# Four or five key tiles of each layer offered to VectorE, and a planner with other durations

## The chip, the cores and the metric

The kernel runs on one core of a Trainium2 chip. The metric is the device time of one execution in microseconds, as the median of several runs. Five engines take part, each with its own instruction queue that it works through in order: TensorE (PE, with its weight loads listed as PEld), VectorE (DVE), ScalarE (ACT), GpSimd (POOL) and SyncE (SP, which issues the DMAs). They wait for each other on semaphores.

## The reference

Two transformer layers with the same weights, over 2048 tokens of width 512, in bfloat16. Each layer is an attention block of 32 heads of 16 and a dense block of width 1792, each behind a layer norm and added to its input:

```python
qkv = (x @ wqkv).reshape(B, S, 3, H, Dh).transpose(2, 0, 3, 1, 4)
q, k, v = qkv[0], qkv[1], qkv[2]
scores = jnp.einsum("bhqd,bhkd->bhqk", q, k) * (Dh ** -0.5)
o = jnp.einsum("bhqk,bhkd->bhqd", softmax(scores), v)
attn = o.transpose(0, 2, 1, 3).reshape(B, S, D) @ wo
dense = gelu(x @ w1 + b1) @ w2 + b2          # gelu by its tanh form
...
x = x + A(layernorm(x)); x = x + B(layernorm(x))     # twice
```

## The kernel before

**The work.** The scores are cut into cells. A cell is the product of 128 keys with 512 query columns of one head: one matmul of 32 rows (two heads share the rows, and the queries of the other head are masked to zero by POOL into `qp`). A pass is one group of four cells per key tile (`a` from 0 to 3, one for each 32-row quarter of PE) over the key tiles of one segment of queries; with all 16 key tiles it has 64 cells. There are 4096 cells in the two layers. For each cell the exponential is taken and the result is multiplied with the values of that head, extended by a column of ones that sums the denominator; the products of a pass add up in PSUM bank 5 (`PVB`). When a pass ends, DVE and POOL divide and transpose its result (`norm`, L718).

**Two ways to an exponential.** PSUM has eight banks of 512 columns. ACT works in two slots, banks 0 to 2 and banks 3 and 4: one score instruction group of PE fills a slot with up to three or two cells, one ACT instruction (L1466) takes the exponential of the whole slot and writes it into as many exp buffers of the `pt` ring, and one value product per cell (L1527) reads it. The ring has `PT_RING` buffers (L24); parts of `k1`, `q` and `v0` join it while they are out of use. Some cells go to DVE instead. DVE turns a score into the bit pattern of a bfloat16 by one multiply and add (`dfirst`, L1283, from banks 6 and 7, or from bank 2). That pattern is a coarse exponential, linear between powers of two. To smooth it, `dchain` makes three more patterns of it, shifted by a fixed number (L1344 makes one, L1346 two; mostly for two cells at once), and all four are multiplied with values: the first with `v`, the other three with copies of it that POOL has scaled by the weights `VW` (`vcopies`, L1060, the instruction on L1068). So a cell on DVE costs four value products, not one. There are nine buffers for cells on DVE (`DU`), and two more late in layer 1.

**Which cells.** `KD` (L45) names for each layer the key tiles whose cells may go to DVE, and `NKD` (L46) sizes the room of the scaled copies. The others always go to ACT; what DVE has not taken by the end of a pass goes to ACT too (`next_act`, L1140). No cell goes to DVE before the scaled copies of all the tiles named for layer 0 are made (`lend` leaves 2 at the end of `vcopies`), nor in the first eight passes, which cover key tiles 0 to 3 alone.

**The order of everything** is made ahead by a list scheduler, `_Sched`, with a model of time. Threads yield operations with a cost in microseconds; the scheduler keeps a clock for each engine, picks the operation that can start first (by priority where several can), and sets its end to start, cost and a latency of its engine (`LATENCY`, L205). A change of PE's mode between scores and the four-way column products (mode "P") costs `SW`. The times themselves do not get into the program, only the order of each engine's queue, and the semaphore waits that the data need. Three decisions are made by the model's clocks when a score instruction is placed: `attach` (L1215) adds cells for DVE to it, if bank 7 or 6 is free within `TOL` of its start and DVE has a buffer; `swap` (L1192) gives the third bank of slot 0 to DVE, if the model's DVE clock is no more than `SWAP` ahead; and the `slack` of a score instruction lets PE run value products ahead of it, as long as it is not held up by more than 0.3 us, or by more where ACT is busy longer with the other slot:

```python
ahead = 0.065 + 0.4267 * self.held[1 - sl]
op = _Op("pe", MM, fns, reads=reads, writes=writes, mode="S", slack=max(SLACK, ahead - LATE))
```

Where PE would stand idle, `fill` (L312) puts in matmuls on the copies whose result nobody reads (L1125); `free` (L1090) chooses the bank that they write to, bank 5 with zero weights among them.

The lines that the prediction speaks of, beside those above: L1137 scores, L512 the projections and the dense block on PE, L683 the copy of projected values into `v`, L734 and L739 to L743 the evacuation of a pass.

Of the kernel before, what the change touches and what calls it, by code (L numbers as in the profile page):

```python
# [20 lines left out]
PVB = 5  # L21
MISC = (6, 7)
DBANK = (7,)
PT_RING = 19  # L24
LEND = (3, 2)
QP_RING = 3
W_RING = 4
# [14 lines left out]
JB = 0.64  # L42
JS = 0.025
EARLY = 4
KD = ((4, 5, 6, 7), (0, 1, 2, 12))  # L45
NKD = 4  # L46
TAIL = 10
OPENING = 18
ROUNDS = 2
# [152 lines left out]
        self.done = False  # L202


LATENCY = {"pe": 0.20, "act": 0.103149, "dve": 0.099491, "pool": 0.153328, "sp": 0.1}  # L205


class _Sched:
# [90 lines left out]
        return max(self.end.get(self.P.lastw[k], 0.0) if k in self.P.lastw else 1e9 for k in keys)  # L299

    def _cost(self, op):
        return op.cost + (SW if op.eng == "pe" and op.mode != self.mode else 0.0)

    def active(self, t):
        while self.stream and self.stream[0][1] < t - WINDOW:
# [6 lines left out]
    def fill(self, start, nxt):  # L312
        while self.filler and self.mode:
# [17 lines left out]
            self.clock["pe"] = now + into + MM + cold  # L331
            self.end[ev] = self.clock["pe"] + LATENCY["pe"]

    def run(self):
        while True:
# [53 lines left out]
            self.clock[e] = start + cost  # L389
            self.end[ev] = start + cost + op.tail + LATENCY[e]  # L390


SW = 0.107
# [3 lines left out]
def bass_interleave_layers__mha_block__dense_activation_gelu__prompt_kernel(  # L397
# [15 lines left out]
    with ExitStack() as es:  # L413
        def sb(shape, dt, name):
            return es.enter_context(nc.sbuf_tensor(name, shape, dt))
# [15 lines left out]
        T["WQKV"] = T["G"][:, 0:12, :].rearrange("p (w c) d -> p w c d", w=3)  # L431
        pt = sb([128, PT_RING, 512], BF16, "pt")
        T["PT"] = [pt[:, :, :]] + [T["K"][1][:, :, 512 * c:512 * c + 512] for c in LEND]
# [10 lines left out]
        T["DU"].append(late.rearrange("p (i j q) -> p i j q", i=4, j=2))  # L444
        T["VC"] = sb([128, NKD, 3, H * 17], BF16, "vc")
        T["XT"] = sb([128, 512], F32, "xt")
# [55 lines left out]
class _Plan:  # L502
# [530 lines left out]
    def setup_attention(self):  # L1033
# [4 lines left out]
        for pi, (l, seg, g, kts, part, final) in enumerate(self.pas):  # L1038
            self.alist.append([(pi, kt, a) for kt in kts if kt not in KD[l] for a in range(4)])
            self.dlist.append([(pi, kt, a) for kt in kts if kt in KD[l] for a in range(4)])  # L1040
            self.left.append(4 * len(kts))
# [18 lines left out]
    def vcopies(self):  # L1060
        T = self.T
        for l in range(NL):
            yield ("cond", lambda l=l: self.pv >= self.lead[l])
            for j, kt in enumerate(KD[l]):
                yield ("need", ("V", l, kt, kt // 4))
# [24 lines left out]
    def free(self, now, ahead):  # L1090
        P = self.P
        best = (None, 1e9)
        src = self.source()
        for b in (6, 7, 0, 1, 2, 3, 4, 5) if src else ():
            k = "B.%d" % b
            if k in ahead or b in self.hold or k in P.lastw and not P.reads.get(k) and P.lastw[k] not in self.s.fills:
                continue
            t = max([0.0] + [self.s.end.get(ev, 0.0) + FOLD for ev in P.deps(src, [k]) if ev[0] != "pe"])
            if max(t, now) < max(best[1], now):
                best = (b, t)  # L1100
        k = "B.%d" % PVB
        if best[1] > now and self.pvopen and "VC.0.0" in P.lastw and k not in ahead:
            best = (PVB, 0.0)
        return best
# [65 lines left out]
    def take(self, c, free):  # L1170
        self.scored += 1
        self.left[c[0]] -= 1
        if self.left[c[0]] == 0:
            free.append(self.s.tokens[("qp", c[0])])

    def join(self, op, d, b, extra, free):
        pools = self.s.pools
        if self.open is None:
            self.open = {"du": pools["du"].pop(0), "cells": [], "full": False}
        pair = self.open  # L1180
        pair["cells"].append(d)
        extra.append((d, b, pair, len(pair["cells"]) - 1))
        if len(pair["cells"]) == self.cap[pair["du"]]:
            self.open = None
        f, r = self.score(d, self.s.tokens[("qp", d[0])], b)
        op.fns.append(f)
        op.reads += r
        op.writes.append("B.%d" % b)
        self.take(d, free)
        self.nd += 1  # L1190
# [141 lines left out]
    def dchain(self, pair):  # L1332
# [16 lines left out]
        for jj, (pi, kt, a) in enumerate(cells):  # L1349
            l, seg, g = self.pas[pi][:3]  # L1350
            gb, ts = self.heads(seg, g)
            j = KD[l].index(kt)
            for i in range(4):
# [26 lines left out]
    def setup_units(self):  # L1380
        self.blocks, self.alias, self.closed = [(0, PT_RING)], {}, set()
        for c in LEND:
            lo = self.blocks[-1][1]
            self.blocks.append((lo, lo + NDC))
            for i in range(NDC):
                self.alias[lo + i] = ["K1.%d.%d" % (i, c)] + ["XL.%d" % t for t in range(4 * c, 4 * c + 4)]
        self.qblocks = len(self.blocks)
        for c in range(self.NQ):
            lo = self.blocks[-1][1]
            self.blocks.append((lo, lo + NDC))  # L1390
            for i in range(NDC):
                self.alias[lo + i] = ["Q.%d.%d" % (i, c)]
        lo = self.blocks[-1][1]
        self.blocks.append((lo, lo + 16))
        for i in range(16):
            self.alias[lo + i] = ["PART.1.%d" % (i // 2)]
# [163 lines left out]
    def run(self):  # L1560
# [6 lines left out]
        s.pool("s", range(len(SLOTS)))  # L1567
        s.pool("pt", range(PT_RING))
        self.setup_units()
# [52 lines left out]
```

## Time and profile before

| | us |
|---|---|
| median of 3 runs (1586.61 to 1589.74) | 1588.72 |
| span of the profiled execution | 1584.3 |
| ACT idle in the span (1584.3 - 1545.8) | 38.5 |
| DVE idle in the span (1584.3 - 1355.7) | 228.6 |
| PE idle in the span (1584.3 - 1432.2) | 152.1 |
| DVE's exponentials: L1283 (du, dh, kt) | 484.5 + 63.0 + 55.5 |
| POOL's scaled copies: 24 of 0.665 | 16.0 |

The profile is one execution on the chip. For each group of instructions it gives the engine, the line, the tiles written and read, the count, the busy time, the mean duration of one, and how long the engine stood idle just before, with what released it. Records of one engine can overlap; busy time counts an overlap once. The records of PE are modelled at their end and overlap most. The granted clock of TensorE is 0.998 on average.

### The profile page before, as it was taken

The page shows a single profiled execution, that of the slowest core. Times are in us where ns is not written, and L with a number is a line of the kernel's source. Part 1 is how long each engine was busy: PE and PEld are TensorE (multiplying, and loading weights), DVE is VectorE, ACT ScalarE, POOL GpSimd, SP SyncE. Part 2 cuts the span into 40 slices and gives each one's busy share as a digit, 9 for nine tenths or more (in the row PEclk, how much of TensorE's full clock was granted, in tenths as well). Part 3 has the DMA queues.
Part 4 walks back from the last instruction along what each step waited for, and adds up shares of the span by engine and source line. Part 5 has one row for each costly group of instructions (what it writes and reads, how often), then busy time and mean ns, then how long its engine had stood idle before and what let it go on. Part 6 is the DMA issues. An engine that isn't in the chain of part 4 may idle for free.

```text
span 1584.3 us, 43090 instructions
## 1 busy us (share of the span) xinstructions
PE 1432.2 (90%) x18795; PEld 447.9 (28%) x18795; DVE 1355.7 (86%) x2558; ACT 1545.8 (98%) x1392; POOL 200.9 (13%) x250
## 2 busy tenths in 40 slices
PE   8998889999999898998989989888898889889988
PEld 3222222222222222322222222222222222333344
DVE  5689999779998889989799789999789978988894
ACT  7999999999999999999999999999999999999995
POOL 5200011010110201002110020122002000010000
PEclk9999999999999999999999999999999999999999
DMA  5100001341014211152111521001251006213420
GB/s 141 22 1 2 1 16 34 95 126 43 22 48 135 80 41 28 42 149 66 35 28 48 159 50 35 1 14 28 84 151 43 26 9 174 82 36 101 142 82 29
DMA packets 141768, 96.90 MB, mean 61 GB/s; under 512 B 36877, under 2 KB 141582, under 8 KB 141582
## 3 DMA queue, kind: packets, MB, share of 16 engines
q1 hardware_dynamic: 141582, 94.14, 21.2%
q8 instruction: 150, 2.46, 0.6%
q14 instruction: 36, 0.29, 0.1%
HBM read 84.41 MB, written 2.10 MB: 55 GB/s over the span
## 4 chain that ended last, share of the span: by engine, by line
ACT 65%; PE 30%; DVE 2%; POOL 1%; DMA 1%; issue 1%; SPq 0%; POOLq 0%; ACTq 0%
ACT pt L1466 58%; PE ps L512 12%; PE ps L1137 9%; PE ps L1527 9%; ACT g L893 2%; ACT v L1466 1%; ACT kt L1466 1%; ACT q L1466 1%; DVE du L1283 1%; ACT L893 1%; PE ps L1125 1%; DMA xf<-xln 1%; DVE du L1346 0%; ACT L1466 0%; DVE du L1344 0%
## 5 line engine op out<-in xcount | busy, mean ns | idle before, releaser
L1466 ACT ACTIVATE pt<-ps 128x1536 bf16<-128x1536 f32 (+1 forms) x1264 | 1387.1, 1259 | 10.5 <-PE ps L1137 6.4
L1137 PE MATMUL ps<-qp,kt 32*128 32x512 bf16 x4096 | 534.7, 384 | 129.9 <-ACT pt L1466 91.5
L1283 DVE TENSOR_SCALAR du<-ps 128x512 uint16<-128x512 f32 x716 | 484.5, 686 | 92.7 <-PE ps L1137 85.9
L1527 PE MATMUL ps<-pt,v 128*17 128x512 bf16 (+1 forms) x3386 | 444.9, 359 | 3.2 <-DVE v L739 1.1
L1137 PEld LDWEIGHTS ps<-qp,kt 32*128 32x128 bf16 x4096 | 141.2, 91 | 677.1 <-ACT pt L1466 286.1
L1527 PE MATMUL ps<-du,vc 128*17 128x512 bf16 (+1 forms) x2403 | 326.6, 359 | 1.3 <-DVE du L1344 0.6
L1346 DVE TENSOR_SCALAR du<-du 128x2048 uint16<-128x2048 uint16 (+1 forms) x361 | 246.7, 686 | 2.2
L1085 POOL TENSOR_SCALAR qp<-q,mask 128x512 bf16<-128x512 bf16 (+1 forms) x91 | 66.9, 735 | 1005.5 <-PE ps L1137 996.4
L512 PE MATMUL ps<-xf,wr 128*32 128x512 bf16 (+1 forms) x2400 | 171.2, 369 | 3.0 <-DMA xf<-xln 1.6
L1344 DVE TENSOR_SCALAR du<-du 128x1024 uint16<-128x1024 uint16 (+1 forms) x361 | 152.6, 433 | 2.2
L1527 PE MATMUL ps<-du,v 128*17 128x512 bf16 (+1 forms) x801 | 148.3, 360 | 0.8 <-DVE du L1346 0.5
L1527 PEld LDWEIGHTS ps<-pt,v 128*17 128x17 bf16 x3386 | 114.4, 88 | 114.8 <-issue 76.6
L512 PE MATMUL ps<-wr,g 128*32 128x512 bf16 x1600 | 123.2, 386 | 3.9 <-ACT g L893 3.2
L1527 PEld LDWEIGHTS ps<-du,vc 128*17 128x17 bf16 x2403 | 91.0, 89 | 65.4 <-issue 30.2
L872 DVE TENSOR_SCALAR g<-ps,hb1t 128x512 bf16<-128x512 f32 (+1 forms) x112 | 79.9, 713 | 15.3 <-PE ps L512 13.9
L1527 PE MATMUL ps<-dh,vc 128*17 128x512 bf16 (+1 forms) x309 | 86.4, 357 | 0.0
L1283 DVE TENSOR_SCALAR dh<-ps 128x512 uint16<-128x512 f32 x92 | 63.0, 685 | 9.3 <-PE ps L1137 7.9
L512 PEld LDWEIGHTS ps<-xf,wr 128*32 128x32 bf16 x2400 | 52.5, 95 | 61.9 <-issue 33.6
L1283 DVE TENSOR_SCALAR kt<-ps 128x512 uint16<-128x512 f32 x81 | 55.5, 685 | 14.9 <-PE ps L1137 13.9
L602 POOL TENSOR_SCALAR xln<-x,rstd,nmr 128x512 bf16<-128x512 bf16 x58 | 56.3, 973 | 30.9 <-DMA xf<-xln 21.6
L1125 PE MATMUL ps<-vc 128*32 128x512 bf16 x520 | 54.7, 384 | 0.0
L754 POOL TENSOR_TENSOR ott<-xt,rc 128x256 bf16<-128x256 f32 x42 | 33.3, 792 | 164.3 <-DVE rc L746 158.8
(93 smaller groups left out, 1184.5 us busy)
## 6 DMA issues: line engine op xcount, KB each, us to landing
wr<-in_B_w_dram SPq DMA_DIRECT2D x256, 256.0 KB, 2.8
wr<-in_A_wqkv_dram SPq DMA_DIRECT2D x24, 256.0 KB, 2.9
wr<-in_A_wo_dram SPq DMA_DIRECT2D x18, 256.0 KB, 2.9
out_dram<-x SPq DMA_DIRECT2D x16, 128.0 KB, 2.6
g<-in_A_wqkv_dram SPq DMA_DIRECT2D x3, 512.0 KB, 6.0
x<-in_A_x_dram SPq DMA_DIRECT2D x3, 512.0 KB, 8.8
q<-in_B_w_dram SPq DMA_DIRECT2D x3, 512.0 KB, 5.5
kt<-in_B_w_dram SPq DMA_DIRECT2D x4, 256.0 KB, 3.3
```

The costliest lines, as they stand in the source:

```text
L512: return [lambda e, a=a: e.matmul(out[32 * a:32 * a + 32, :], lhsT=lhsT[:, 32 * a:32 * a + 32], rhs=rhs, start=start, stop=stop, tile_posi ...
L602: yield _Op(eng, cost, lambda e: e.tensor_scalar(T["XLN"][:, x, :], T["X"][:, t, :], T["RSTD"][:, t:t + 1], T["NMR"][:, t:t + 1], op0=ALU. ...
L872: yield _Op("dve", 0.21 + n / 966, lambda e, fc=fc, pb=pb: e.tensor_scalar(T["G"][:, fc, q], pb, T["HB1T"][:, fc:fc + 1], None, op0=ALU.ad ...
L893: lambda e, g=g: e.activation(out=g, in_=g, func=ACT.Gelu_apprx_tanh), reads=gk, writes=gk, prio=2)
L1085: yield _Op("pool", 0.1 + 0.6 * w / 512, lambda e, s=s, q=q, i=i, t=t, w=w: e.tensor_scalar(T["QP"][:, s, w * i:w * i + w], q, T["MASK"][: ...
L1125: fns.append(lambda e, o=o, w=w, a=a, m=m: e.matmul(o, lhsT=w, rhs=rhs, start=start, stop=start, tile_position=(0, m * a)))
L1137: return (lambda e: e.matmul(o, lhsT=lhsT, rhs=rhs, start=True, stop=True, tile_position=(32 * a, 0)), ["K%d.%d.%d" % (l, gb, kt // 4), "Q ...
L1283: yield _Op("dve", 0.68, lambda e: e.tensor_scalar(u, self.bank(b), E_SCALE, E_BIAS, op0=ALU.mult, op1=ALU.add), reads=["B.%d" % b], write ...
L1344: yield _Op("dve", 0.08 + 0.14 * n, lambda e: e.tensor_scalar(U[:, 1, 0:n, :], U[:, 0, 0:n, :], SHIFT, None, op0=ALU.add), reads=key[0], w ...
L1346: yield _Op("dve", 0.08 + 0.28 * n, lambda e: e.tensor_scalar(U[:, 2:4, 0:n, :], U[:, 0:2, 0:n, :], 2 * SHIFT, None, op0=ALU.add), reads=k ...
L1466: yield _Op("act", 0.065 + 0.4267 * n, lambda e, src=src, dst=dst: e.activation(out=dst, in_=src, func=ACT.Exp, scale=0.25), reads=["B.%d" ...
L1527: op.fns.append(lambda e, o=o, lhsT=q[0][0][m], rhs=q[0][1][:, n * m:n * m + n], a=a, st=st, sp=sp: e.matmul(o, lhsT=lhsT, rhs=rhs, start= ...
```

## The change

The planner gets other durations: larger latencies for PE, ACT and DVE; 0.083 us less for each DVE operation (at least 0.07 is left); 2% more for a PE operation of mode "P". A fifth key tile of each layer may go to DVE: tile 8 in layer 0, tile 3 in layer 1. Its three scaled copies take 3 x 544 x 2 = 3264 bytes of each partition; three buffers of the exp ring, 3 x 1024 = 3072 bytes, are given up. In `free`, bank 5 is no longer in the list of banks that filler matmuls may take; the rule behind the loop, which allows bank 5 in the middle of a pass, stays.

```diff
-PT_RING = 19
+PT_RING = 16
...
-KD = ((4, 5, 6, 7), (0, 1, 2, 12))
-NKD = 4
+KD = ((4, 5, 6, 7, 8), (0, 1, 2, 3, 12))
+NKD = 5
...
-LATENCY = {"pe": 0.20, "act": 0.103149, "dve": 0.099491, "pool": 0.153328, "sp": 0.1}
+LATENCY = {"pe": 0.219, "act": 0.21, "dve": 0.139, "pool": 0.153328, "sp": 0.1}
+OVERLAP = 0.083
+ROUND = 1.02
...
     def _cost(self, op):
-        return op.cost + (SW if op.eng == "pe" and op.mode != self.mode else 0.0)
+        if op.eng == "dve":
+            return max(op.cost - OVERLAP, 0.07)
+        if op.eng == "pe":
+            return op.cost * (ROUND if op.mode == "P" else 1.0) + (SW if op.mode != self.mode else 0.0)
+        return op.cost
...
-        for b in (6, 7, 0, 1, 2, 3, 4, 5) if src else ():
+        for b in (6, 7, 0, 1, 2, 3, 4) if src else ():
```

## The prediction

> **What bounds the kernel now.** I read the page's busy shares first, then its chain, its groups of instructions, the stretches by engine, the engines' own timelines and last the list of waits. The page's head and its chain:
>
> ```profile
> span 1584.3 us, 43090 instructions
> PE 1432.2 (90%) x18795; PEld 447.9 (28%) x18795; DVE 1355.7 (86%) x2558; ACT 1545.8 (98%) x1392; POOL 200.9 (13%) x250
> ...
> ACT 65%; PE 30%; DVE 2%; POOL 1%; DMA 1%; issue 1%; SPq 0%; POOLq 0%; ACTq 0%
> ```
>
> ACT is at work in all but 38.5 us of the span, and most of the chain runs on it. So the time is ACT's work plus its few gaps, and only a cell taken from ACT shortens it. The groups say where cells go (line, engine, operation, tiles and count; busy us and mean ns of one; idle before it and its releaser):
>
> ```profile
> L1466 ACT ACTIVATE pt<-ps 128x1536 bf16<-128x1536 f32 (+1 forms) x1264 | 1387.1, 1259 | 10.5 <-PE ps L1137 6.4
> L1137 PE MATMUL ps<-qp,kt 32*128 32x512 bf16 x4096 | 534.7, 384 | 129.9 <-ACT pt L1466 91.5
> L1283 DVE TENSOR_SCALAR du<-ps 128x512 uint16<-128x512 f32 x716 | 484.5, 686 | 92.7 <-PE ps L1137 85.9
> L1346 DVE TENSOR_SCALAR du<-du 128x2048 uint16<-128x2048 uint16 (+1 forms) x361 | 246.7, 686 | 2.2
> L1344 DVE TENSOR_SCALAR du<-du 128x1024 uint16<-128x1024 uint16 (+1 forms) x361 | 152.6, 433 | 2.2
> ```
>
> There are 4096 score cells. L1283, the first step of a cell on DVE, runs 716 times into du, 92 into dh, 81 into kt: 889 cells, of 1024 that four key tiles offer. ACT takes the other 3207. DVE stands idle 107.7 us ahead of L1283 (85.9 + 13.9 + 7.9 in the three groups), always for a score: it isn't given cells as fast as it could take them. The stretches (us, then busy time and count of PE, PEld, DVE, ACT, POOL; clock; DMA share; GB/s):
>
> ```profile
> 80.00:1540.00 1460.00, 1320.91 (x17094) 402.97 (x17091) 1286.31 (x2409) 1448.22 (x1290) 166.99 (x194) 1.00 0.22 61
> ...
> 200.00:300.00 100.00, 92.32 (x1083) 26.46 (x1080) 93.47 (x177) 98.30 (x90) 12.67 (x13) 1.00 0.11 30
> 300.00:400.00 100.00, 92.84 (x1167) 27.29 (x1169) 82.10 (x151) 99.63 (x91) 10.16 (x12) 1.00 0.34 96
> ```
>
> In the middle, 80 to 1540 us, DVE is busy 88% and ACT 99%. But DVE reaches 93% in one stretch shown (94.24 between 1000 and 1100) and 82% in the next; that difference is the room.
>
> **Why the planner leaves it: its DVE is too slow.** The timeline of DVE (start, us, operation):
>
> ```profile
> 824.79 0.68 DVE L1346 TENSOR_SCALAR du<-du 128x2048 uint16<-128x2048 uint16 x1
> 825.39 0.68 DVE L1283 TENSOR_SCALAR kt<-ps 128x512 uint16<-128x512 f32 x1
> 825.99 0.41 DVE L1344 TENSOR_SCALAR du<-du 128x1024 uint16<-128x1024 uint16 x1
> 826.32 0.68 DVE L734 COPY v<-ps 128x512 f32<-128x512 f32 x1
> ```
>
> Each starts some 0.08 us before the record of the one ahead ends: L1346 and L1283 hold DVE 0.60 under records of 0.68, L1344 0.33 under 0.41. A cell costs DVE 0.60 + (0.33 + 0.60)/2 = 1.065 us (L1344 and L1346 serve two cells). The old plan books 0.68 + (0.36 + 0.64)/2 = 1.18, the new one 0.597 + (0.277 + 0.557)/2 = 1.014. So the plan goes from 11% too dear to 5% too cheap. Over all 2558 operations it books 2558 x 0.083 = 212 us less, against 229 us that DVE is idle in fact: the old plan's DVE is nearly full, and that is what holds the count of cells at 889.
>
> One rule speaks against this: the Trainium skill, VectorE: DVE Perf Modes, section "The DRAIN you can't avoid", has the next operation not start until the pipe is empty, though it adds that one that is not held starts earlier. With whole records a cell would cost 1.25 us, the new plan would be 19% too cheap, and the same room would hold 52 cells, a gain of 23 us; the starts above decide for the overlap.
>
> **The change part by part.**
>
> *DVE's cost less 0.083.* A saturated plan hands out more cells. How many, no trace of before shows. Below: none, if the score banks (6, 7 and the swapped bank 2) or the nine exp buffers of DVE hold the count. Above: DVE busy all of the middle, (1460 - 1286.3)/(1.065 + 0.44) = 115, where each cell also shortens the middle by 0.44. I take what the fullest stretches already reach, 94%: (0.94 x 1460 - 1286.3)/(1.065 + 0.94 x 0.44) = 58 cells. The price on ACT comes from its timeline:
>
> ```profile
> 1201.45 1.59 ACT L1466 ACTIVATE q<-ps 128x1536 bf16<-128x1536 f32 x1
> 1202.78 1.18 ACT L1466 ACTIVATE pt<-ps 128x1024 bf16<-128x1024 f32 x1
> 1203.69 1.62 ACT L1466 ACTIVATE q<-ps 128x1536 bf16<-128x1536 f32 x1
> 1205.02 10.25 ACT L1466 ACTIVATE pt<-ps 128x1024 bf16<-128x1024 f32 x9
> ```
>
> Three banks take 1.33 us from start to start, two take 0.91: 0.42 a cell, 0.07 an instruction. At 2.4 cells each a cell is worth 0.42 (swapped) to 0.45 (attached); I use 0.44. **58 x 0.44 = -25.6 us** (0 to -50.6).
>
> *Five key tiles.* They offer 1280 cells. Without them a pass of 64 would stop at 16: the middle's 874 + 58 cells in 1434 us are 65 per 100 us, while passes of some 24 us at 16 cells allow 66. So this part makes room for the first and has no time of its own. Its six more V copies (L1068, 665 ns each) are 4 us on a POOL that is busy 13%. Layer 0's fifth tile is 8, of the third chunk; no cell goes to DVE before its copies. V tile 8 is written at 54.1, three copies end at about 57, and the first L1283 starts at 66.1: 9 us of cover. Without it, each us late costs 0.6 of a cell, 0.3 us.
>
> *More value products.* Each moved cell adds three, 174 in all; a round of four takes about 0.21 us of PE, so 9 us. Some 24 score instructions fall away. PE has 139 us free in the middle and 100 us of fillers (L1125) there, which give way. Cost 0; if that cover were gone, 9.
>
> *Exp buffers 19 to 16.* ACT waited 1.5 us in all for a value product to free one (of its 10.5 above). Between 0 and ten times that; I take +1, nearer the small end, since five tiles also leave ACT fewer cells to buffer. What is late next in such a wait is the score of the slot behind it.
>
> *Latencies (ACT 0.103 to 0.21, PE 0.20 to 0.219, DVE 0.099 to 0.139).* PE runs its queue in order. The planner now holds a slot's banks for ready 0.107 later, and may put value products ahead of the refill. In the list of waits (us, times, longest):
>
> ```profile
> PEld ps L1137 <- ACT pt L1466: 286.1, 576, 1.5
> ...
> PE ps L1137 <- ACT pt L1466: 91.5, 239, 1.0
> PE ps L1137 <- DVE du L1283: 10.1, 18, 1.0
> ```
>
> 576 of 1333 refills already stand at PE before ACT is done. Those are the ones that could come later: filling that wait is free, overshooting it stalls ACT, and behind a late refill both the next exp and everything queued on PE wait. Only refills of three banks behind a two-bank exp of 0.91 us are tight: 541 x 576/1333 x 0.107 = 25 us if all of it shows, 0 if none does. ACT's scant 6.4 us of waits for scores speak for the low end: +5. A plan that waits less on PE could also gain, but ACT's gaps outside the opening and the close are under 12 us in all, so that is at most -5, within the range.
>
> *PE's round x 1.02 and no filler into bank 5 ahead of a pass.* The clock is 1.00 in these stretches with the old fillers, and the second way into bank 5 stays. 0, or up to +3 if PE cools; more value products take the fillers' place.
>
> **Sum.** Span 1584.3 - 25.6 + 1 + 5 = 1564.7. The median of the runs, 1588.7, is 4.4 above this execution's span; with it **1569 us** (1.2% less).
>
> **The rivals.** *DVE filled to the brim:* 115 cells, -50.6, and twice the stalls, +12: 1550. For it: 5% too cheap a DVE and ample cells. Against: nine buffers and two banks turn round no faster than score, wait and 0.60 allow. *The change does not move cells:* banks and buffers hold DVE, 0 to 15 more, -3 with +2 of stalls: 1587. For it: DVE's 82% stretches, which a full model DVE alone doesn't explain. Against: DVE's waits are for scores, not for PE's order of value products. *Slower, by refills that come late:* a DVE booked 5% too cheap runs behind the plan, banks 2 and 7 come free late, and PE, in order, holds the scores behind them, on top of the 0.107. Price: 541 three-bank refills x 0.107 = 58 us, less 25.6: 1621. It outweighs the gain from 47 ns a refill on. For it: PE's 92% in the stretch 200 to 300 and the 18 waits on L1283 already there. Against: at 94% DVE still catches up.
>
> **How the numbers follow.** Forecast 0.58 (own range 1556 to 1584); filled 0.12; no cells moved 0.13; late refills 0.17. A change under 0.2%, 3.2 us, can't be told from none here. Faster: 0.58, 0.12 and half of the third, 0.76. Same: 0.05 from the third and 0.02 from the last, 0.07. Slower: 0.15 and 0.02, 0.17. Range 1546 to 1596: below it lies a third of the filled case, above it most of the last.
>
> **What would show it.** L1283 in du, dh and kt counts 930 to 970; ACT's cells 3207 less the same; DVE over 90% in the middle; idle before L1283 well under 107.7. Wrong if L1283 stays under 900, or if ACT's idle before L1466 grows from 10.5 us past 35; a growing wait of L1137 on L1283 would name the last rival.

## The result, and the profile after

The changed kernel takes 1611.51 us (1610.53 to 1613.25), the kernel before beside it 1587.94: a ratio of 1.0157, 95% interval 1.0137 to 1.0178. It is 1.6% slower, where 1.2% faster was forecast. The page of the changed kernel; its lines stand six further down than before, so L1289, L1350 and L1352 are DVE's three steps, L1143 the scores, L1472 ACT's exponentials and L1533 the value products:

```profile
span 1610.2 us, 43408 instructions
PE 1436.7 (89%) x18835; PEld 438.2 (27%) x18835; DVE 1425.8 (89%) x2731; ACT 1525.6 (95%) x1370; POOL 215.0 (13%) x256
...
DVE 48%; PE 28%; ACT 20%; POOL 2%; issue 1%; DMA 1%; SPq 0%; ACTq 0%; DVEq 0%
...
L1472 ACT ACTIVATE pt<-ps 128x1024 bf16<-128x1024 f32 (+1 forms) x1150 | 1256.2, 1191 | 48.8 <-PE ps L1143 39.1
L1289 DVE TENSOR_SCALAR du<-ps 128x512 uint16<-128x512 f32 x777 | 517.8, 681 | 72.6 <-PE ps L1143 70.5
...
L1289 DVE TENSOR_SCALAR dh<-ps 128x512 uint16<-128x512 f32 x101 | 68.7, 680 | 2.2 <-PE ps L1143 2.2
L1289 DVE TENSOR_SCALAR kt<-ps 128x512 uint16<-128x512 f32 x92 | 62.6, 680 | 6.8 <-PE ps L1143 6.3
```

The work did move: L1289 runs 777 + 101 + 92 = 970 times, 81 more than before, and ACT is busy 20.2 us less (1545.8 to 1525.6). But ACT now stands idle 84.6 us of the span where it was 38.5. The two make the span's difference: -20.2 + 46.1 = +25.9. (81 cells at the 0.44 of the prediction would have been -35.6. Busy time counts an overlap of records once, and where an exp is no longer followed at once, the end of its record, 0.13 to 0.17 us for L1472 in these traces, is no longer shared with the next. ACT's records leave 260 gaps where they left 127; 133 more of these ends are 17 to 23 us by this estimate, which covers the difference.) The chain that ended last has changed engines: DVE's share of it was 2%, and is 48%.

The list of waits says how DVE, busy only 89%, holds ACT (waiting engine, tile and line, what it waited for; us, times, longest):

```profile
PE ps L1143 <- ACT pt L1472: 52.8, 124, 1.5
PE ps L1143 <- DVE du L1289: 36.4, 74, 1.5
PE ps L1143 <- DVE dh L1289: 8.8, 15, 2.7
PE ps L1143 <- DVE kt L1289: 7.3, 12, 1.3
...
ACT pt L1472 <- PE ps L1143: 39.1, 90, 2.0
ACT kt L1472 <- PE ps L1143: 4.6, 8, 2.1
ACT q L1472 <- PE ps L1143: 3.1, 5, 1.6
ACT v L1472 <- PE ps L1143: 0.9, 3, 0.4
```

The lines of the kernel before that go with these, beside the 91.5, the 10.1 and the 6.4 that the prediction shows:

```profile
PE ps L1137 <- DVE kt L1283: 2.5, 4, 0.8
PE ps L1137 <- DVE dh L1283: 1.5, 2, 1.1
ACT kt L1466 <- PE ps L1137: 0.5, 2, 0.3
```

PE's scores wait 52.5 us for the first step of a cell on DVE, which frees their bank; before it was 14.1. Their waits on ACT fell from 91.5 to 52.8: PE more often comes to a score with ACT already done, and finds DVE late. ACT in its turn waits 47.7 us for scores where it waited 6.9, and these 40.8 us are most of the 46.1 that its idle time grew by. One place in order of time, first the chain that ended last (start, us, what), then the timeline of all engines at its end:

```profile
227.24 0.69 DVE x L791
227.93 0.60 DVE du L1289
228.53 0.60 DVE du L1352
229.13 0.60 DVE du L1289
229.73 0.34 DVE dh L1352
230.07 0.67 DVE du L1350 x2
...
255.43 0.60 DVE du L1352
256.03 1.80 DVE du L1289 x3
257.82 0.61 DVE dh L1289
258.43 0.04 issue
258.48 0.42 PE ps L1143 x4
258.90 0.02 issue
258.92 1.46 ACT pt L1472
```

```profile
255.95 1.88 DVE L1289 TENSOR_SCALAR du<-ps 128x512 uint16<-128x512 f32 x3
...
257.74 0.68 DVE L1289 TENSOR_SCALAR dh<-ps 128x512 uint16<-128x512 f32 x1
...
258.48 0.61 PE L1143 MATMUL ps<-qp,kt 32*128 32x512 bf16 x6 [0.55 <-DVE dh L1289]
258.92 2.37 ACT L1472 ACTIVATE pt<-ps 128x1536 bf16<-128x1536 f32 x2 [0.69 <-PE ps L1143]
```

From 227 to 258 us the chain stays almost wholly on DVE, which works through its queue with hardly a gap and at the 0.60, 0.34 and 0.60 us that the trace of before had shown. At the end of it a score instruction of PE waits 0.55 us for DVE to take a cell out of a bank, and the exp behind that score leaves ACT idle 0.69 us. Elsewhere DVE waits for scores in its turn (70.5 us ahead of L1289 into du). So DVE is the bound in stretches like this one, and not over the whole span.

### The profile page after: what moved, and what is told of

It reads as the page before. It is cut to its first block, busy times and chain, and to the rows that moved or that the text cites. A ratio compares the mean times of both kernels' runs of the same rounds, so it can differ in the third digit from the quotient of the medians.

```text
span 1610.2 us, 43408 instructions
## 1 busy us (share of the span) xinstructions
PE 1436.7 (89%) x18835; PEld 438.2 (27%) x18835; DVE 1425.8 (89%) x2731; ACT 1525.6 (95%) x1370; POOL 215.0 (13%) x256
## 4 chain that ended last, share of the span: by engine, by line
DVE 48%; PE 28%; ACT 20%; POOL 2%; issue 1%; DMA 1%; SPq 0%; ACTq 0%; DVEq 0%
DVE du L1289 17%; ACT pt L1472 14%; PE ps L518 10%; PE ps L1533 9%; DVE du L1352 9%; PE ps L1143 9%; DVE du L1350 5%; ACT g L899 2%; DVE dh L1289 2%; DVE g L878 2%; DVE kt L1289 2%; DVE stats L587 2%; ACT v L1472 1%; DVE dh L1352 1%; DMA xf<-xln 1%
## 5 line engine op out<-in xcount | busy, mean ns | idle before, releaser
L1472 ACT ACTIVATE pt<-ps 128x1024 bf16<-128x1024 f32 (+1 forms) x1150 | 1256.2, 1191 | 48.8 <-PE ps L1143 39.1
L1143 PE MATMUL ps<-qp,kt 32*128 32x512 bf16 x4096 | 531.8, 388 | 125.6 <-ACT pt L1472 52.8
L1289 DVE TENSOR_SCALAR du<-ps 128x512 uint16<-128x512 f32 x777 | 517.8, 681 | 72.6 <-PE ps L1143 70.5
L1533 PE MATMUL ps<-pt,v 128*17 128x512 bf16 (+1 forms) x2996 | 437.6, 364 | 5.3 <-DVE v L745 1.6
L1533 PE MATMUL ps<-du,vc 128*17 128x512 bf16 (+1 forms) x2601 | 352.6, 364 | 5.3 <-DVE du L1352 4.5
L1143 PEld LDWEIGHTS ps<-qp,kt 32*128 32x128 bf16 x4096 | 136.3, 91 | 667.2 <-DVE du L1289 186.7
L1352 DVE TENSOR_SCALAR du<-du 128x2048 uint16<-128x2048 uint16 (+1 forms) x393 | 271.4, 694 | 4.1
L1350 DVE TENSOR_SCALAR du<-du 128x1024 uint16<-128x1024 uint16 (+1 forms) x393 | 164.5, 428 | 4.7
L1533 PE MATMUL ps<-du,v 128*17 128x512 bf16 (+1 forms) x867 | 161.4, 365 | 6.6 <-DVE xt L749 2.2
L1533 PEld LDWEIGHTS ps<-pt,v 128*17 128x17 bf16 x2996 | 110.1, 89 | 107.6 <-issue 67.6
L1533 PEld LDWEIGHTS ps<-du,vc 128*17 128x17 bf16 x2601 | 95.0, 90 | 69.3 <-issue 28.6
L1533 PE MATMUL ps<-dh,vc 128*17 128x512 bf16 (+1 forms) x339 | 97.5, 366 | 0.5 <-DVE du L1352 0.4
L1472 ACT ACTIVATE kt<-ps 128x1536 bf16<-128x1536 f32 (+1 forms) x66 | 89.9, 1365 | 6.0 <-PE ps L1143 4.6
L1533 PE MATMUL ps<-kt,v 128*17 128x512 bf16 (+1 forms) x299 | 76.3, 368 | 0.3 <-DVE v L745 0.2
L1472 ACT ACTIVATE v<-ps 128x1536 bf16<-128x1536 f32 (+1 forms) x53 | 69.8, 1327 | 2.3 <-PE ps L1143 0.9
L1289 DVE TENSOR_SCALAR dh<-ps 128x512 uint16<-128x512 f32 x101 | 68.7, 680 | 2.2 <-PE ps L1143 2.2
L1289 DVE TENSOR_SCALAR kt<-ps 128x512 uint16<-128x512 f32 x92 | 62.6, 680 | 6.8 <-PE ps L1143 6.3
```

Source lines behind the costliest of these rows:

```text
L1143: return (lambda e: e.matmul(o, lhsT=lhsT, rhs=rhs, start=True, stop=True, tile_position=(32 * a, 0)), ["K%d.%d.%d" % (l, gb, kt // 4), "Q ...
L1289: yield _Op("dve", 0.68, lambda e: e.tensor_scalar(u, self.bank(b), E_SCALE, E_BIAS, op0=ALU.mult, op1=ALU.add), reads=["B.%d" % b], write ...
L1350: yield _Op("dve", 0.08 + 0.14 * n, lambda e: e.tensor_scalar(U[:, 1, 0:n, :], U[:, 0, 0:n, :], SHIFT, None, op0=ALU.add), reads=key[0], w ...
L1352: yield _Op("dve", 0.08 + 0.28 * n, lambda e: e.tensor_scalar(U[:, 2:4, 0:n, :], U[:, 0:2, 0:n, :], 2 * SHIFT, None, op0=ALU.add), reads=k ...
L1472: yield _Op("act", 0.065 + 0.4267 * n, lambda e, src=src, dst=dst: e.activation(out=dst, in_=src, func=ACT.Exp, scale=0.25), reads=["B.%d" ...
L1533: op.fns.append(lambda e, o=o, lhsT=q[0][0][m], rhs=q[0][1][:, n * m:n * m + n], a=a, st=st, sp=sp: e.matmul(o, lhsT=lhsT, rhs=rhs, start= ...
```

## The experiments

Two theories were stated at first, with a third beside them. **Booking:** the planner now books DVE too short, hands it more than it can do in time, and PE's queue, which runs in order, waits on it. **Refill:** the larger latencies with an unchanged slack let scores come late. **Buffers:** three exp buffers fewer starve ACT. The table has all runs: the median, the ratio to the kernel before with its interval, the cells on DVE, ACT's waits for scores, PE's score waits for DVE's first step (us, summed over the tiles), and the granted clock of the profiled execution.

| run | median us | ratio [95%] | cells | ACT on scores | PE on DVE | clock |
|---|---|---|---|---|---|---|
| before | 1587.9 | | 889 | 6.9 | 14.1 | 0.998 |
| changed | 1611.5 | 1.0157 [1.0137, 1.0178] | 970 | 47.7 | 52.5 | 0.985 |
| e1 overlap 0 | 1615.4 | 1.0172 [1.0147, 1.0197] | 895 | 19.3 | 8.8 | 0.981 |
| e2 old latencies | 1617.5 | 1.0187 [1.0164, 1.0209] | 968 | 45.8 | 45.9 | 0.989 |
| e3 four tiles | 1608.7 | 1.0128 [1.0107, 1.0148] | 950 | 43.5 | 43.7 | 0.994 |
| e4 chain right | 1589.4 | 1.0012 [1.0, 1.0024] | 964 | 19.1 | 23.3 | 0.996 |
| e5 cost alone | 1609.9 | 1.0151 [1.013, 1.0172] | 953 | 45.1 | 49.4 | 0.988 |
| e6 latencies alone | 1597.7 | 1.0082 [1.0061, 1.0103] | 903 | 15.5 | 5.3 | 0.996 |
| e7 tiles alone | 1599.5 | 1.0086 [1.0071, 1.0102] | 894 | 8.7 | 7.9 | 0.996 |
| e8 chain right, old latencies | 1587.9 | 1.0013 [1.0003, 1.0022] | 960 | 16.7 | 29.8 | 0.997 |
| e9 and four tiles | 1588.3 | 1.001 [0.9999, 1.0021] | 945 | 21.0 | 37.2 | 0.997 |
| e10 buffers alone | 1604.8 | 1.0103 [1.0086, 1.012] | 888 | 10.6 | 11.2 | 0.993 |
| e11 scatter, DVE | 1602.1 | 1.0096 [1.007, 1.0122] | 888 | 14.1 | 7.5 | 0.993 |
| e12 scatter, PE | 1592.2 | 1.0026 [1.0012, 1.0041] | 892 | 9.1 | 9.0 | 0.994 |
| e13 changed, sibling | 1622.4 | 1.022 [1.0199, 1.0242] | 971 | 44.6 | 50.6 | 0.990 |
| e14 pick, four tiles | 1569.2 | 0.9895 [0.988, 0.991] | 942 | 10.8 | 23.4 | 0.996 |
| e15 pick, five tiles | 1579.0 | 0.9958 [0.9942, 0.9974] | 949 | 17.0 | 24.6 | 0.995 |
| e16 pick, most cells | 1581.7 | 0.9977 [0.9963, 0.9991] | 977 | 24.1 | 28.3 | 0.992 |
| e17 more fillers | 1607.9 | 1.0139 [1.0107, 1.0172] | 972 | 41.1 | 49.1 | 0.994 |
| e18 round and bank 5 | 1608.4 | 1.0141 [1.0109, 1.0173] | 977 | 44.1 | 45.0 | 0.997 |

**First group: one part of the change undone, or mended.**

e1, on the changed kernel:

```diff
-OVERLAP = 0.083
+OVERLAP = 0.0
```

> The changed kernel with OVERLAP at 0, the rest of the change kept. Booking theory (DVE's operations are booked shorter than they run, the plan overfills DVE, and PE's queue waits on it): about 895 cells on DVE, ACT's waits for scores back under 20 us, 1585 to 1595. Refill theory (the larger latencies with an unchanged slack let refills come late): no cure here, ACT's waits stay near 45 us, and with 75 cells fewer on DVE the time rises to 1620 or more. Buffer theory (three exp buffers fewer): 1605 or more.

1615.4 us. PE's waits on DVE are gone (8.8), ACT's waits for scores fell to 19.3, and the time did not: a miss for booking, which alone doesn't explain this run. ACT waits 18.7 us for value products here to free a buffer, 1.5 before. The rest of the change has a price of its own when DVE gives nothing for it.

e2, on the changed kernel:

```diff
-LATENCY = {"pe": 0.219, "act": 0.21, "dve": 0.139, "pool": 0.153328, "sp": 0.1}
+LATENCY = {"pe": 0.20, "act": 0.103149, "dve": 0.099491, "pool": 0.153328, "sp": 0.1}
```

> The changed kernel with the old LATENCY, the rest kept. Booking theory: DVE is as overfull as before, 1605 to 1620. Refill theory: the refills are placed as in the kernel before, ACT's waits for scores under 20 us, 1575 to 1585.

1617.5 us: a miss for refill, which falls as the explanation of the loss. PE's 45.9 us on DVE and ACT's 45.8 on scores stay.

e3, on the changed kernel:

```diff
-PT_RING = 16
+PT_RING = 19
...
-KD = ((4, 5, 6, 7, 8), (0, 1, 2, 3, 12))
-NKD = 5
+KD = ((4, 5, 6, 7), (0, 1, 2, 12))
+NKD = 4
```

> The changed kernel with four key tiles and 19 exp buffers, the new model of time kept. Booking theory: some 950 cells on DVE, nearly as overfull, 1600 to 1612. Buffer theory: the stalls go with the three buffers back, 1580 or less.

1608.7 us with 950 cells, as booking said. ACT waits for no value product at all in this run, so the buffers aren't it either. And four tiles give 950 cells.

e4, on the changed kernel, the two operations that `dchain` yields:

```diff
-        yield _Op("dve", 0.08 + 0.14 * n, ...
+        yield _Op("dve", OVERLAP + 0.066 + 0.134 * n, ...
...
-        yield _Op("dve", 0.08 + 0.28 * n, ...
+        yield _Op("dve", OVERLAP + 0.068 + 0.266 * n, ...
```

> The changed kernel with the chain's two operations (make one shifted pattern, make two) booked at 0.334 and 0.600 us for two cells and 0.200 and 0.334 for one, as they start apart in the trace, in place of 0.277, 0.557, 0.137 and 0.277. Booking theory: the error was in these, some 964 cells on DVE and a DVE that keeps up with its plan, ACT's waits for scores under 25 us, 1570 to 1585, faster than before. Refill or buffer theory: within 8 us of the changed kernel's 1611.

1589.4 us, 22 less than the changed kernel, with 964 cells against 970 and everything else of the change in place. The old costs of these two, 0.36 and 0.64 us for two cells, already lay close to the 0.334 and 0.600 at which the operations start apart; it is the records that overlap by 0.083, and they last 0.43 and 0.69. Taking the overlap off the old costs took it off twice. The gain stopped at the kernel before, though, and did not reach 1585: against it ACT is busy 22.3 us less (1523.5) and idle 26.4 us more (64.9), and only 12.2 of these 26.4 are waits for scores. The page and the waits of this run:

```profile
DVE 41%; PE 32%; ACT 24%; POOL 1%; issue 1%; DMA 1%; SPq 0%; ACTq 0%
...
PE ps L1143 <- ACT pt L1472: 62.5, 152, 1.7
PE ps L1143 <- DVE du L1289: 19.8, 46, 1.3
```

DVE still leads the chain, but PE's waits on L1289 have halved (36.4 to 19.8 for this tile).

**Second group: one part alone, on the kernel before.** e5 takes 0.083 off every DVE operation in `_cost`, e6 has the new `LATENCY`, e7 the five tiles and 16 buffers; e8 is e4 with the old `LATENCY`.

```diff
     def _cost(self, op):
+        if op.eng == "dve":
+            return max(op.cost - 0.083, 0.07)
         return op.cost + (SW if op.eng == "pe" and op.mode != self.mode else 0.0)
```

> The kernel before with 0.083 us less for every DVE operation of the planner, and nothing else of the change. Booking theory: some 953 cells on DVE and the same stalls as the changed kernel, PE's waits on DVE above 35 us, 1600 to 1615. If the other parts were needed for the loss: 1575 or less, since 64 cells more on DVE are worth 28 us.

1609.9 us: DVE's cost by itself makes a loss as large as the whole change, with the same waits (49.4 and 45.1).

> The kernel before with the new LATENCY alone. After the run with OVERLAP at 0, which stayed at 1615 with 895 cells, the latencies must cost something by themselves: refill theory says 1600 to 1612, ACT's gaps up by 15 us or more with DVE's cells near 903. Booking theory alone says 1582 to 1590.

1597.7 us, between the two. ACT's waits for scores rose by 8.6 us, with PE's waits on DVE lower than before.

> The kernel before with five key tiles and 16 exp buffers alone. Booking theory: the count stays at some 894 cells, since DVE is full in the plan, and the time within 5 us of 1588. Buffer theory: ACT's waits on value products (1.5 us before) above 10 us, 1598 or more.

1599.5 us. The count of cells stays at 894, as the prediction had it: with the old booking a fifth tile brings none. The time is the one that the buffer theory gave, and ACT's waits on value products are 13.3 us, so the buffers seem to have a price here.

> The changed kernel with the chain's operations booked as they start apart in the trace, and the old LATENCY. Refill theory: some 960 cells and fewer late refills than with the new latencies (1589), 1565 to 1580, faster than both kernels. Booking theory alone: 1585 to 1593, as the run with the chain alone.

1587.9 us: a miss for refill. With the chain right, the latencies hardly matter (1589.4 with the new ones).

All three parts lose alone, 11 to 24 us. That every change to this kernel should lose was suspicious, so the third group asks what a change that means nothing does.

**Third group: the scatter of plans.** e9 has both mends, the old latencies and four tiles. e10 is the kernel before with `PT_RING = 16`. e11 and e12 alter one figure of the model by less than half a per cent:

```diff
-DV = 0.69
+DV = 0.688
```

```diff
-MM = 0.2132140802823403
+MM = 0.2133
```

> The changed kernel with the chain booked as it runs, the old LATENCY, four key tiles and 19 exp buffers: of the change, only the cheaper DVE (and PE's round and bank 5) is left, with the right figure for the chain. Booking theory with the buffers' price: some 945 cells, ACT's waits on value products from 15 back to under 4 us, 1568 to 1580, faster than both kernels. If the buffers' waits are only the scatter of plans: 1583 to 1592.

1588.3 us; the waits on value products did fall, from 16.4 in e8 to 4.3, and the time stayed. The 1588 of three runs is no floor set by the buffers.

> The kernel before with 16 exp buffers alone. Buffer theory: ACT's waits on value products 8 us or more, 1594 to 1602, as with five tiles and 16 buffers (1599.5). Scatter theory: anywhere within 10 us of 1588, with no such waits.

1604.8 us, with these waits of ACT, 1.5 us before for the first line (with 3.6 more into v, the waits on value products are 14.3):

```profile
ACT pt L1466 <- PE ps L1527: 10.7, 9, 2.9
ACT pt L1466 <- PE ps L1137: 10.0, 25, 0.8
```

> The kernel before with evacuations on DVE booked at 0.688 in place of 0.690 us: a change of the model too small to mean anything, so that another plan of the same quality comes out. If plans scatter: 3 to 15 us from 1588. If they don't: within 3 us.

1602.1 us, 15 slower than the kernel before for 0.002 us of one figure.

> The kernel before with a round of PE booked at 0.2133 in place of 0.2132 us, a second plan of the same quality. If plans scatter: 3 to 15 us from 1588, and not by the same amount as with DVE's figure. If they don't: within 3 us.

1592.2 us, 5 slower. So the order that the scheduler finds hangs on the last digit of its costs, and the plan of the kernel before is better than both of these siblings. Any new plan, good or bad in its parts, is measured against a lucky one. What e6, e7 and e10 lose (11, 13 and 18 us) is of the size of this scatter; their parts have visible waits, but their price isn't settled by one plan each.

**Fourth group: is the loss scatter too, and is it the cells?** e13 is the changed kernel with `DV = 0.688`. e14 to e16 have the chain as in e4 and other figures in the model; each was picked from several hundred such plans, as one whose queues fit well when every operation is given the duration that the traces show. The core of e14, against the changed kernel:

```diff
-LATENCY = {"pe": 0.219, "act": 0.21, "dve": 0.139, "pool": 0.153328, "sp": 0.1}
-OVERLAP = 0.083
+LATENCY = {"pe": 0.200, "act": 0.147, "dve": 0.125, "pool": 0.153328, "sp": 0.1}
+OVERLAP = 0.072
...
-SLACK = 0.3
-LATE = 0.7
+SLACK = 0.26
+LATE = 0.68
```

with `PT_RING`, `KD` and `NKD` as before the change.

> The changed kernel with evacuations on DVE booked at 0.688 in place of 0.690 us before the overlap: another plan of the same quality as the changed kernel's. Booking theory: 970 cells and 1603 to 1620, above the siblings of the kernel before (1592, 1602). Scatter theory (the changed kernel is an unlucky plan): 1585 to 1600.

1622.4 us, 2 above the range of booking and far from that of scatter: the changed kernel's 1611.5 wasn't bad luck.

> The chain booked as it runs, the overlap at 0.072, latencies between the old and the new (ACT 0.147, DVE 0.125, PE 0.2), slack 0.26 and 0.68, four key tiles and 19 exp buffers; picked from several hundred such plans as the one whose queues fit best with the durations that the traces show. Booking and scatter together: some 942 cells, ACT idle near 55 us, 1570 to 1580, faster than both kernels. If picking is of no use, 1588 as the three plans with the right chain so far.

1569.2 us, ratio 0.9895 [0.988, 0.991]: faster than both kernels. Its page:

```profile
span 1566.9 us, 43266 instructions
PE 1418.9 (91%) x18804; PEld 440.0 (28%) x18804; DVE 1388.2 (89%) x2681; ACT 1525.4 (97%) x1382; POOL 201.8 (13%) x250
...
ACT 39%; PE 35%; DVE 23%; POOL 1%; DMA 1%; issue 1%; SPq 0%; ACTq 0%
...
L1472 ACT ACTIVATE pt<-ps 128x1024 bf16<-128x1024 f32 (+1 forms) x1244 | 1353.3, 1227 | 15.8 <-PE ps L1143 10.8
```

ACT is busy as long as in the changed kernel (1525.4 against 1525.6) and idle 41.5 us against 84.6. So a plan can keep most of what the moved cells save, with 942 cells of the 1024 that four tiles offer. But e14 differs from e9 both in its figures (overlap, latencies, slack) and in being picked, and no run separates the two; and that its 1569 us is the figure of the forecast is chance, since it is another plan with other figures.

> A second pick, with five key tiles and 16 exp buffers, overlap 0.077, latencies 0.196 for ACT, 0.133 for DVE and 0.21 for PE, slack 0.22 and 0.68, and swaps only where DVE's clock is 0.3 ahead or less: some 949 cells, 1570 to 1582. The buffers' price would show as waits of ACT on value products of 5 us or more.

1579.0 us, within the expectation, with 5.6 us of waits on value products.

> A third pick, with five key tiles and the most cells: overlap 0.078, latencies 0.207 for ACT, 0.139 for DVE and 0.2 for PE, slack 0.29 and 0.73: some 977 cells, 1570 to 1585. If it is the number of cells on DVE that overloads it, 1600 or more, as the changed kernel with its 970.

1581.7 us with 977 cells, seven more than the changed kernel (this pick has `ROUND` at 1.0 too): the number of cells alone does not make the loss. With e4, whose 964 cells differ from the changed kernel's 970 by the one edit to the chain, this leaves what the planner believes about the time that they take.

**Last group: the clock, and the parts not yet undone.** Five of the slower plans also show a lower clock, 0.981 to 0.990. e17 is the changed kernel with `WARM = 0.45` in place of 0.38, e18 has `ROUND = 1.0` and bank 5 back among the banks of fillers.

> The changed kernel with more filler matmuls (the planner puts them in below a PE activity of 0.45, not 0.38): some 308 groups in place of 216, 972 cells. Clock theory (a PE held up by DVE idles, its granted clock falls to 0.985, and the slow scores cost the time): the clock back at 0.995 or more and 1590 to 1600. Booking theory: the clock recovers but PE's waits on L1289 stay above 40 us and the time at 1603 to 1618.

```profile
PE ps L1143 <- ACT pt L1472: 45.4, 116, 1.3
PE ps L1143 <- DVE du L1289: 36.6, 82, 1.8
```

The clock is back at 0.994, PE's waits are those of the changed kernel (36.4 for the second line), and the time is 1607.9: most of the loss stays without the low clock.

> The changed kernel with the last parts undone, PE's round at 1.0 and bank 5 among the banks of fillers. If these two matter: under 1600. Booking theory: some 977 cells and 1603 to 1622.

1608.4 us at a clock of 0.997: these two parts are not the cause either, and the low clock is not the main one.

The clock does have a share. Executions of one and the same kernel differ in it: the 61 of the kernel before that ran beside the experiments go from 1582.4 us at 1.000 to 1592.9 at 0.991, on average 0.75 us for each 0.001. The changed kernel's four have 0.985 to 0.988 where these have 0.995 on average, so by this slope, an estimate, some 7 of its 24 us go with the clock. The rest do not: the executions of e3, e5, e17 and e18 at 0.994 or more take 1606 to 1608 us, and those of the kernel before at 0.994 to 0.997 take 1585 to 1587 on average. Nor do PE's stalls by themselves set the clock, since e3 and e18 have them at 0.994 and 0.997.

## Why the prediction was wrong

*What bounds the kernel, and why DVE is not given more cells:* right. The count rose from 889 to 970 as soon as DVE's costs fell (e5: 953 by the costs alone), and not by more tiles alone (e7: 894).

*"58 x 0.44 = -25.6":* the term held in its mechanism. There were 81 cells, ACT's busy time fell by 20.2, and e14 shows that a plan can keep it. Three of the signs that the prediction named held as well: 930 to 970 cells, DVE over 90% busy in the middle (1354.55 of the 1485 us from 80 to 1565, 91%), and its idle time for scores ahead of its first step well under 107.7 us (79.0).

*The step that failed is the wait of scores on DVE, for which the sum enters nothing.* The prediction had worked out, from the starts in the trace, that the new model books a cell at 1.014 us and DVE takes 1.065, "5% too cheap", and then let that figure count only in the rivals, with "Against: at 94% DVE still catches up". The one term for late scores, +5, was put down to the latencies. DVE does not catch up: PE's scores wait 38.4 us more for it (14.1 to 52.5), and ACT's waits for scores rose by 40.8 us (6.9 to 47.7) where 5 were entered. Two of the signs that the prediction gave for its being wrong came: ACT's idle time before its exponentials into pt went from 10.5 to 48.8 us, past the 35 named, and the growing wait of scores on DVE's first step "would name the last rival". Three pairs of runs that differ in the chain's booking show the cause: e4 against the changed kernel -22, e8 against e2 -30, e9 against e3 -20 (this pair differs in the latencies too). So do all the plans taken together: the seven that book the chain too short (changed, e2, e3, e5, e13, e17, e18) take 1608 to 1622 us with 41 to 48 us of ACT's waits for scores, and the six that book it as it runs (e4, e8, e9, e14 to e16) take 1569 to 1589 with 11 to 24. The error that e4 mends sat in L1344 and L1346: "0.277 + 0.557" for operations that the same paragraph had timed at 0.33 and 0.60. A reading that fits is that a plan which takes an engine for free when it isn't puts that engine's results just ahead of where others need them, and the in-order queue of PE passes each delay on; the planner's own times, which would show it directly, are in no run.

*The rival that was given 0.17, "Slower, by refills that come late",* named the mechanism: DVE behind the plan, banks late, PE in order. What it had wrong is the price. It took 541 refills by the 0.107 of ACT's new latency, 1621 us; the latencies are not what delays them (e2, 1617.5 without them), and what the scores wait for is DVE's first step. That 1621 lies near the 1611.5 measured is therefore luck.

*A second assumption stood nowhere in the sum: that a new plan is as good as the old one apart from its parts.* e11 and e12 show siblings of it that are 15 and 5 us worse for a changed digit. This alone would have eaten a quarter to three quarters of the 20 us that were forecast, and it may be why the three plans with the right chain that nobody picked (e4, e8, e9) stop at 1588.

*"+1" for the exp buffers:* mis-sized where ACT has most of the cells (e10: 14.3 us of waits on value products, e7: 13.3, against 1.5 before), nearer in the changed kernel (5.5). The time that they cost isn't settled, since scatter is as large.

*"Without them a pass of 64 would stop at 16":* the limit is there, since four tiles of four cells are 16, but it does not bind at this count: the prediction's own 65 cells per 100 us lie under its 66. Four tiles gave 950 cells in e3 and 942 in e14, the fastest of all, where the forecast stood for 889 + 58 = 947. The fifth tile was not needed.

*"Cost 0" for the value products, and the V copies' cover:* right. PE's busy time rose by 4.5 us and L1289 starts at 66.3, against 66.1 before. *"Up to +3 if PE cools":* it did cool, to 0.985, which by the slope within one kernel goes with some 7 us. No run shows the 3; e17 and e18, at 0.994 and 0.997, are 3 to 4 us faster than the changed kernel, inside the scatter.

What stays open: the price of the latencies and of the buffers by themselves, for which several plans of each would be needed; and why e1, with DVE booked as before, loses as much as the changed kernel. Its waits (18.7 us on buffers, 19.3 on scores) look like those two prices added, and its clock, 0.981 to 0.986, is the lowest of all, but no run separated these. So the loss of the changed kernel is shown to go with the chain's booking when the rest of the change is in place (e4) and to come with DVE's booking alone (e5); that undoing all of DVE's booking cures it is not shown (e1).

## What to carry to other kernels

When a planner's costs are set to a trace, take for each kind of operation the distance from start to start in a full queue, and take nothing off a cost that was already of that kind: some 0.05 us too little on each of the chain's 1082 operations cost 22 us here (e4), more than the 20.2 us that 81 cells moved off the busiest engine took from its work. For an engine that others wait for, an error towards too cheap can be worse than a larger one towards too dear: 5% too cheap gave 1608 to 1622 us in seven plans, 11% too dear gave 1588 to 1605 in six, with e1 at 1615 as the exception. And before a part of such a change is judged, run the same plan with a meaningless digit altered: if that moves the time by 5 to 15 us, single plans tell little below that. Picking among many may be worth as much as the change was meant to bring: the three picks lie 5 to 17 us under the kernel before, though their figures differ too.

## What the runs showed of the hardware

DVE's overlap is real and steady: an operation starts some 0.08 us before the record of the one ahead ends, in every kernel here, with a median of 0.080 to 0.083 us. Busy time counts each overlap once, so the share by records overstates how full DVE is by that tail at each gap alone: 612 gaps after, some 51 us, which makes the 89% about 85% (an estimate from these counts). And yet DVE was the bound in stretches.

Some operations of the chain take far longer than their kind. In the changed kernel's listing of L1352 (duration in ns: least, median, most), and in the timelines of DVE and of POOL:

```profile
L1352 DVE TENSOR_SCALAR du<-du x393: 355/686/2719, 71.1 to 1575.0; 128x2048 uint16<-128x2048 uint16 x195, 128x1024 uint16<-128x1024 uint16 x2
```

```profile
252.20 1.11 DVE L1352 TENSOR_SCALAR du<-du 128x2048 uint16<-128x2048 uint16 x1
```

```profile
251.52 2.68 POOL L608 TENSOR_SCALAR xln<-x,rstd,nmr 128x512 bf16<-128x512 bf16 x2 [0.30 <-DVE nmr L597]
```

In the records of the trace, 27 of the chain's 1082 operations last over 0.8 us, and each of the 27 overlaps an instruction of POOL in time; in the kernel before it is 31 of 990, again all of them. The Trainium skill, SBUF — State Buffer, section "Who interferes with whom", has VectorE in its two-port modes and GpSimd exclude each other, whichever comes first. The rows agree in that operations last longer beside POOL's and nowhere else, but only some of those that lie beside them do (27 of 233), and which mode they ran in, no run shows. The time over 0.69 us adds up to 8.4 us after and 6.8 before, too little to make the difference.
